# Loads, evictions and matmul order in the head of a fused attention and feed-forward kernel: a second piece of a weight matrix sent from ScalarE, small weights and the last rows of the input loaded later

## The chip, the cores and the metric

The kernel runs on one core of one Trainium2 chip. The metric is the time of one execution on the device in microseconds; three runs were made of the kernel before, and one more execution was profiled.

A core has five engines with a queue of instructions each: TensorE (in the profile PE, its weight loads PEld), VectorE (DVE), ScalarE (ACT), GpSimd (POOL) and SyncE (SP). Each works through its queue in order. SyncE, ScalarE and GpSimd can issue DMAs. An instruction that needs another engine's result, or a landed DMA, waits for a semaphore, and all that is queued behind it on its engine waits too.

## What is computed

One layer on 2048 rows of 448 columns: a normalisation, then a linear attention with 16 heads of 28 columns and a feed-forward part side by side, both added to the input.

```python
xn = _layernorm(x, axis=-1)
return x + _A_ref(xn, A_wqkv, A_w_phi, A_wo) + _B_ref(xn, B_w1, B_w2)

# _A_ref
qkv = (x @ wqkv) ...                       # 16 heads of 28 columns
pq = einsum("bhsd,hdf->bhsf", q, w_phi);  pk = the same of k
phi = concatenate([softmax(p), softmax(-p)])   # of pq and of pk
kv = einsum("bhsf,bhsd->bhfd", phi_k, v);  z = sum of phi_k
o = (phi_q @ kv) / (phi_q @ z + 1e-6);  return o @ wo

# _B_ref
return silu(x @ w1) @ w2                   # 448 -> 1792 -> 448
```

## The kernel before

The program is written as a list of operations with their dependencies. A planner inside the kernel (`schedule`) puts the operations of each engine in order by estimated times; `chain([...])` forces the order of named operations of one engine, and the order of TensorE after the head is written out by hand in `PLAN`. Waits are derived from the dependencies when the instructions are emitted.

**Tiles.** The rows are 16 tiles of 128 (numbers 0 to 15), grouped by four for the feed-forward part (chunks 0 to 3). For each tile `ln_tile` emits the statistics (`bnst`, `bnag`, DVE, L702 and L703), the root of the variance (`ve`, and `rstd`; on ScalarE and DVE for tiles 0 to 3, on POOL for the others, L711 and L713) and the normalisation `xn` (DVE, L717). The normalised tile is then needed with its columns across the partitions. Tiles 0 to 3 are turned on TensorE (`tr0a tr0 tr1 tr2 tr3`, L537) and evicted by ScalarE (`ev0a ev0 ev1 ev2`, L543) or DVE (`ev3`, L547). Tiles 4 to 15 are turned in pairs by DMA transposes from SyncE (`xnT_dma5` for tiles 4 and 5, to `xnT_dma15`).

**The head** is what TensorE does until the first three blocks of the feed-forward part have been fed from tiles 0 to 3: 16 transposes of 128 columns and 72 matmuls of 128 columns. A word such as 01a is block 0, tile 1, part a; part a is the first two steps of the contraction (4 matmuls), part b the third (2 matmuls), and without a letter all three. Blocks 0 and 1 need columns 0 to 511 of `w1`: rows 0 to 255 of it (`w1_0`) for part a, the others (`w1_0r`) for part b. Block 2 needs columns 512 to 1023: rows 0 to 383 (`w1_512`), and for its last matmul of each tile the others (`w1_512r`). `w1` is kept in a part of the tile phT, so its loads are called phT<-in_B_w_dram. Before the head 38 matmuls on ones warm TensorE up (L586).

**After the head** the words of `PLAN` follow: r0, r1, r2 finish the first three blocks; aF and bF are the two halves of a feed-forward block (F7 to F13 are of chunk 1, F21 to F27 of chunk 3), with six and eight matmuls of 512 columns on half of the rows each; av/bv, ak/bk and aq/bq are blocks of the projections; f0 and f1 multiply the map weights `w_phi` into the weights of k (`fold_k`), g0 and g1 into those of q. A fold needs the block-diagonal copies `BD` and `BD0` of the map weights (`bdphi`, `bd0`, POOL, L632 and L636), which come from the loads `wphi` to `wphi3` (issued by POOL, L557), and the transposed weights `wT_dma0` to `wT_dma8` (DMA transposes from SyncE). Its results are read out of two banks by ScalarE (`fold_ref`, last_k) and DVE (`fold_sub`, Wqk, L695). f0 and f1 use the same two banks (6 and 7), so f1 waits for the `fold_sub` of f0.

**Queues around the change.** SyncE issues x0, x1, x2, `w1_0`, `w1_0r`, `w1_512r`, x4, the last third of `w1`, `wv`, x8, then the transposes; ScalarE issues `w1_512` after its first table load. POOL runs its memsets, issues the four loads of the map weights, stands at `bdphi` until they have landed, and goes on with `ve4`.

```python
        chain("bnst0 bnag0 bnst1 bnag1 rstd0 xn0a xn0 rstd1 xn1 bnst2 bnag2 bnst3 bnag3 rstd2 xn2 rstd3 xn3 ev3".split())
        chain("warm_act w1_512 ve0 ve1 ev0a ev0 ev1 ve2 ve3 ev2 silu_table".split())
```

Of the kernel before, what the change touches and what calls it, by code (L numbers as in the profile page):

```python
# [8 lines left out]
ACTF = mybir.ActivationFunctionType  # L9
# [349 lines left out]
SIGNAL = {("act", "pe"): 60.0, ("act", "dve"): 40.0, ("dve", "pe"): 100.0, ("dve", "sp"): 30.0, ("dve", "dve"): 34.0,  # L359
          ("pool", "pe"): 100.0}  # L360
PLAN = """r0 aF3@4 r2 r1 bF3 aF6@0 aF4@6 bF6 bF4 aF5@4 av2@2 av0@0 bv2 bF5 av4@6 bv0 bv4 aF10@2 aF9@0 bF10 f0@6 bF9 aF12@4 aF7@2
aF11@0 f1@6 bF11 bF7 bF12 aF25@0 ak2@6 bF25 bk2 av8@4 av12@2 bv8 ak0@0 bv12 bk0 av10@6 aF22@4 bv10 aF17@2 bF22 av14@6
aF14@0 bF17 bv14 aF18@4 bF14 aF27@6 ak4@2 bF27 bF18 bk4 av6@6 ak6@0 ak8@4 bv6 bk8 bk6 ak12@2 aF8@6 bk12 bF8 aY0@45
aF21@0 aY0 aF23@2 bF21 bF23 ak14@6 bY0 g0@1 bk14 bY0 aF13@0 aF19@2 bF13 aF20@4 bF19 aF24@6 bF20 bF24 ak10@0 g1@3 bk10 K0
K6 K4 aq4@2 K12 aq8@4 bq4 K8 K2 s4 aq0@0 bq8 aq6@2 K14 bq0 bq6 bY1@45 K10 M aY1 aq2@2 aF26@0 s6 bq2 bY1 bF26 aG3@23 aY1
aU2@67 s8 aF15@0 bU2 s0 bF15 aF16@4 bG3 bF16 aU4@01 aq12@6 bU4 bq12 aU3@45 bG3 bU3 s2 aG3 aq10@0 aq14@6 bq10 s10 aW2@45
# [5 lines left out]
def bass_parallel_sum__linear_kernel_hedgehog__dense_activation_silu__prompt_kernel(  # L372
# [10 lines left out]
    S, D, H, DH, FF = 2048, 448, 16, 28, 1792  # L383
# [25 lines left out]
    with es:  # L409
# [38 lines left out]
        w1_sb = flat[:, 0:4 * FF].rearrange("p (k f) -> p k f", k=4)  # L448
# [27 lines left out]
        warm_act = sb("warm_act", [128, 4], F32)  # L476
# [25 lines left out]
        P = _Prog()  # L502
# [96 lines left out]
        def load_w1(c0, c1, eng="sp"):  # L599
            load_rows4(w1_sb[:, :, c0:c1], B_w1, c0, c1, f"w1_{c0}", eng)  # L600
# [2 lines left out]
        load_x(1, 2)  # L603
        load_x(2, 4)
        load(w1_sb[:, 0:2, 0:512], B_w1[0:256, 0:512].rearrange("(k p) f -> p k f", p=128), "w1_0")
        load(w1_sb[:, 2:4, 0:512], bass.AP(B_w1.tensor, B_w1.offset + 256 * FF, [[FF, 128], [64 * FF, 2], [1, 512]]), "w1_0r")
        load_w1(512, 1024, "act")
        load_x(4, 8)
        load_w1(1024, FF)
        load_rows4(wv_sb, A_wqkv, 2 * D, 3 * D, "wv")  # L610
# [88 lines left out]
        def ln_tile(t):  # L699
            xs = x_sb[:, t, :]  # L700
            sl = t % NXN
            P.op("dve", 590, lambda e: e.bn_stats(st6[:, t, :], xs), reads=[xs], writes=[st6[:, t, :]], name=f"bnst{t}", okeys_w=["ln"])  # L702
            P.op("dve", 170, lambda e: e.bn_aggr(mv[:, t, :], st6[:, t, :]), reads=[st6[:, t, :]], writes=[mv[:, t, :]], name=f"bnag{t}",  # L703
                 okeys_w=["ln"])
            if t < 4:
                P.op("act", 220, lambda e: e.activation(ve[:, t:t + 1], mv[:, t, 1:2], ACTF.Sqrt, bias=epst[:]),
                     reads=[mv[:, t, 1:2], epst[:]], writes=[ve[:, t:t + 1]], name=f"ve{t}", table="sqrt", okeys_r=["sq"])
                P.op("dve", 120, lambda e: e.reciprocal(rstd[:, t:t + 1], ve[:, t:t + 1]),
                     reads=[ve[:, t:t + 1]], writes=[rstd[:, t:t + 1]], name=f"rstd{t}")
            else:  # L710
                P.op("pool", 200, lambda e: e.tensor_scalar(ve[:, t:t + 1], mv[:, t, 1:2], EPS_LN, None, ALU.add),  # L711
                     reads=[mv[:, t, 1:2]], writes=[ve[:, t:t + 1]], name=f"ve{t}")
                P.op("pool", 570, lambda e: e.tensor_tensor(rstd[:, t:t + 1], ve[:, t:t + 1], neghalf[:], ALU.pow),  # L713
                     reads=[ve[:, t:t + 1], neghalf[:]], writes=[rstd[:, t:t + 1]], name=f"rstd{t}")

            def norm(dst, c0, c1, dur, tag=""):
                P.op("dve", dur, lambda e: e.tensor_scalar(dst, x_sb[:, t, c0:c1], mv[:, t, 0:1], rstd[:, t:t + 1], ALU.subtract, ALU.mult),  # L717
                     reads=[xs, mv[:, t, 0:1], rstd[:, t:t + 1]], writes=[dst], name=f"xn{t}{tag}")

            dstx = xnT[:, t, :, :]  # L720
            if t >= XN_DMA0:
                norm(xn_sb[:, sl, 0:KF], 0, KF, 370)
                norm(xn_sb[:, sl, KF:512], D - 128, D, 250)
                if t % 2:
                    dma_t(xnT[:, t - 1:t + 1, :, :].rearrange("p i k c -> p (i k) c"),
                          xn_sb[:, sl - 1:sl + 1, :].rearrange("p i c -> p (i c)"), 950.0, f"xnT_dma{t}", 1330.0, lat=850.0)
                return

            def turn_over(k0, k1, b, tag):
                tps = bank16[b][:, 128 * k0:128 * k1].rearrange("p (k c) -> p k c", k=k1 - k0)  # L730
                transposes([(tps[:, kt - k0, :], xn_sb[:, sl, KS[kt]:KS[kt] + 128]) for kt in range(k0, k1)], f"tr{tag}")
                if t < 3:
                    act(dstx[:, k0:k1, :], tps, ACTF.Identity, 128 * (k1 - k0), f"ev{tag}")
                else:
                    copy(dstx[:, k0:k1, :], tps, 128 * (k1 - k0), f"ev{tag}")

            if t == 0:
                norm(xn_sb[:, sl, 0:256], 0, 256, 290, "a")
                norm(xn_sb[:, sl, 256:D], 256, D, 275)
                turn_over(0, 2, 4, "0a")  # L740
                turn_over(2, 4, 5, "0")
            else:
                norm(xn_sb[:, sl, 0:D], 0, D, 390)
                turn_over(0, 4, (7, 4, 5)[t - 1], str(t))

        LOW, HIGH = slice(0, 64), slice(64, 128)

# [266 lines left out]
        def chain(names):  # L1014
            byname = {o.name: o for o in P.ops}
            for a, b in zip(names, names[1:]):
                byname[b].odeps.add(byname[a].id)
                byname[b].odeps -= byname[b].deps
# [3 lines left out]
            ln_tile(t)  # L1022
        fold()
        act(warm_act[:], ones_bf[:, 0:4], ACTF.Silu, 4, "silu_table", table="silu", okeys_w=["sq"])
        chain("bnst0 bnag0 bnst1 bnag1 rstd0 xn0a xn0 rstd1 xn1 bnst2 bnag2 bnst3 bnag3 rstd2 xn2 rstd3 xn3 ev3".split())
        chain("warm_act w1_512 ve0 ve1 ev0a ev0 ev1 ve2 ve3 ev2 silu_table".split())
        byname = {o.name: o for o in P.ops}
        byname["w1_512"].deps.add(byname["warm_act"].id)
        byname["w1_512"].odeps -= byname["w1_512"].deps
        fold_loads()  # L1030

        chunk = [(fp, c) for c in range(NCH) for fp in range(FP)]
# [3 lines left out]

        head = [F(0, 0), F(1, 2), F(2, AUX)]
        seq = []
        for word in "tr0a tr0 tr1 00a 10a 01a 11a 00b 10b 01b 11b tr2 20 21 tr3 02 12 22 03 13 23".split():
            if word[0] == "t":  # L1040
                seq.append(word)
                continue
            f, t = int(word[0]), int(word[1])
            n0 = len(P.ops)
            head[f][0](t * 128, t * 128 + 128, {"": (0, 1, 2), "a": (0, 1), "b": (2,)}[word[2:]])
            for n, o in enumerate(P.ops[n0:]):
                o.name = f"F{word}_{n}"
                seq.append(o.name)
# [4 lines left out]
        block_mask(mask2[:], 2 * DH, 2, KP)  # L1053
        memset(vaug[:, :, :, DH], 1.0, 2150, "vaug1")
        memset(KVm[:], 0.0, 464, "kvm0")
        chain(["vaug1", "kvm0", "wphi", "wphi1", "wphi2", "wphi3"])
        def k_block(t, b0):
            return proj_block(t, b0, True)

# [35 lines left out]
        for word in PLAN.split():  # L1095
# [36 lines left out]
                    finish_pair(t, bank_of[t])  # L1132
            elif kind == "f":
                fold_k(*map(int, arg.split("@")))
            elif kind == "g":
                fold_q(*map(int, arg.split("@")))
            elif kind == "K":
                t0 = int(arg)
                kv(range(t0, t0 + 2))
                if t0 < NEK:  # L1140
                    ones_column(t0, t0 + 2)
            elif kind == "M":
                kvm()
# [111 lines left out]
```

## Time and profile before

| what | value |
|---|---|
| median of the 3 runs | 146.27 us (146.14 to 146.69) |
| the profiled execution, whole | 146.72 us |
| its span, first to last instruction | 145.5 us |
| busy: PE, DVE, ACT, POOL | 97%, 62%, 55%, 52% of the span |
| granted TensorE clock | 1.000 |
| first transposes of the head on PE | 5.07 us |
| r0, the first matmuls after the head | 11.5 us |
| last slices of the span, DMA for the output | PE 0.4 busy in the last fortieth |

The span is counted from the first instruction of the program, and all times of the timeline are microseconds from there. The 1.2 us between the profiled execution and its span lie before the first and after the last instruction. In the page's 40 slices a digit is the busy share in tenths, one slice being 3.64 us:

```profile
PE   7989999899999999999999999999999999999994
DVE  1957899610770059948139999927796374635533
ACT  4567856379997899979896949246530000000000
POOL 8807477720097007799944999992398600000000
DMA  4999969654990000000000059959989999743522
```

### The profile page before, as it was taken

To read this page: it belongs to the slowest core of one execution; us is meant where nothing else is said; L and a number is where in the kernel's file an instruction comes from. 1 tells how busy PE (TensorE), PEld (TensorE's weight loads), DVE (VectorE), ACT (ScalarE), POOL (GpSimd) and SP (SyncE) were. 2 spreads that over 40 slices of the span, in tenths; PEclk is the share of its full clock that TensorE was granted. 3 is DMA by queue.
4 is the path that set the end of the run, shared out by engine and by line. 5 is a ranking of instruction groups with operands and counts; after the bars stand their busy time and mean duration, and the time that the engine had idled before them with its cause. 6 is when DMAs were issued, how large, how long until landed. Compare 5 with 4: busy or idle time off the path is not lost.

```text
span 145.5 us, 4553 instructions
## 1 busy us (share of the span) xinstructions
PE 141.3 (97%) x1968; PEld 83.0 (57%) x1968; DVE 89.5 (62%) x195; ACT 79.5 (55%) x96; POOL 75.2 (52%) x95
## 2 busy tenths in 40 slices
PE   7989999899999999999999999999999999999994
PEld 7785444345444544477787655555555556555773
DVE  1957899610770059948139999927796374635533
ACT  4567856379997899979896949246530000000000
POOL 8807477720097007799944999992398600000000
DMA  4999969654990000000000059959989999743522
GB/s 103 346 342 264 266 142 138 133 106 68 337 293 7 0 2 5 0 0 5 0 5 5 0 89 179 137 109 181 76 163 171 206 196 176 117 76 72 165 95 63
DMA packets 44500, 17.59 MB, mean 121 GB/s; under 512 B 36912, under 2 KB 44096, under 8 KB 44480
## 3 DMA queue, kind: packets, MB, share of 16 engines
q1 hardware_dynamic: 41648, 15.09, 53.0%
q10 hardware_dynamic: 2704, 2.19, 5.4%
q8 instruction: 15, 0.25, 0.7%
q0 software_dynamic: 128, 0.03, 0.1%
q14 instruction: 5, 0.04, 0.1%
HBM read 6.57 MB, written 1.84 MB: 58 GB/s over the span
## 4 chain that ended last, share of the span: by engine, by line
PE 68%; DVE 18%; POOL 5%; DMA 4%; issue 3%; ACT 1%; DVEq 0%; POOLq 0%; ACTq 0%
PE psum L520 68%; DVE Rec L837 7%; DMA Wp<-in_A_w_phi_dram 4%; DVE RA L717 4%; DVE st L702 3%; DVE Rec L838 2%; POOL rstd L713 1%; POOL Wp L557 1%; DVE mv L703 1%; POOL vaug L550 1%; DVE Wqk L695 1%; ACT Ek_sb L543 1%; POOL ve L711 1%; POOL BD L632 0%; DVE Y_sb L949 0%
## 5 line engine op out<-in xcount | busy, mean ns | idle before, releaser
L520 PE MATMUL psum<-xnT,phT 64*128 64x512 bf16 (+1 forms) x428 | 46.9, 350 | 0.6 <-DMA phT<-in_B_w_dram 0.4
L520 PE MATMUL psum<-w_sb,hT 64*128 64x448 bf16 (+4 forms) x455 | 46.5, 341 | 0.0
L837 DVE TENSOR_REDUCE Rec<-Ek_sb 128x32 f32<-128x896 bf16 (+1 forms) x20 | 24.4, 1251 | 18.7 <-ACT Ek_sb L543 18.6
L543 ACT ACTIVATE hT<-psum 128x1024 bf16<-128x1024 f32 x28 | 27.7, 1024 | 11.3 <-PE psum L520 11.2
L520 PEld LDWEIGHTS psum<-w_sb,hT 64*128 64x128 bf16 (+1 forms) x455 | 23.6, 94 | 17.2 <-issue 0.2
L520 PEld LDWEIGHTS psum<-xnT,phT 64*128 64x128 bf16 (+1 forms) x428 | 22.4, 95 | 19.0 <-DMA phT<-in_B_w_dram 0.6
L874 POOL TENSOR_TENSOR RA<-Ek_sb,Rec 128x896 bf16<-128x896 bf16 x16 | 27.1, 1723 | 5.7 <-DVE Rec L838 4.9
L520 PE MATMUL psum<-Wqk,xnT 64*128 64x432 bf16 x224 | 24.4, 342 | 0.0
L543 ACT ACTIVATE Ek_sb<-psum 128x864 bf16<-128x864 f32 x24 | 20.3, 917 | 6.3 <-PE psum L520 4.2
L847 POOL TENSOR_TENSOR Ek_sb<-Ek_sb,Rec 128x896 bf16<-128x896 bf16 x8 | 13.4, 1698 | 17.8 <-DVE Rec L838 17.8
L520 PEld LDWEIGHTS psum<-Wqk,xnT 64*128 64x128 bf16 x224 | 11.1, 94 | 8.2
L543 ACT ACT_TABLE_LOAD x11 | 14.1, 1283 | 1.0 <-PEq L1240 0.8
L847 POOL TENSOR_TENSOR phT<-phT,Rec 128x896 bf16<-128x896 bf16 x8 | 13.4, 1700 | 1.5 <-issue 0.9
L520 PE MATMUL psum<-wv,xnT 64*128 64x448 bf16 x112 | 12.2, 349 | 0.0
L1001 DVE TENSOR_TENSOR x_sb<-psum,x_sb 128x448 bf16<-128x448 f32 (+2 forms) x13 | 7.2, 583 | 7.5 <-PE psum L520 7.4
L702 DVE BATCH_NORM_STATS2 st<-x_sb 128x6 f32<-128x448 bf16 x16 | 9.7, 604 | 3.1 <-DMA x_sb<-in_A_x_dram 3.1
L520 PE MATMUL psum<-wo_sb,vaug 64*128 64x448 bf16 (+2 forms) x102 | 11.3, 338 | 0.0
L717 DVE TENSOR_SCALAR RA<-x_sb,mv,rstd 128x384 bf16<-128x384 bf16 (+4 forms) x29 | 9.0, 349 | 2.3 <-POOL rstd L713 2.1
L980 DVE TENSOR_TENSOR vaug<-psum,rden 128x448 bf16<-128x448 f32 x16 | 9.2, 619 | 0.0
L837 DVE TENSOR_REDUCE Rec<-phT 128x64 f32<-128x1792 bf16 x4 | 8.0, 1990 | 1.8 <-ACT phT L543 1.8
L838 DVE RECIPROCAL Rec<-Rec 128x32 f32<-128x32 f32 (+1 forms) x24 | 8.8, 396 | 0.2
L520 PEld LDWEIGHTS psum<-wv,xnT 64*128 64x128 bf16 x112 | 5.4, 94 | 5.6 <-ACT vaug L543 0.5
(60 smaller groups left out, 108.9 us busy)
## 6 DMA issues: line engine op xcount, KB each, us to landing
out_dram<-x_sb ACTq DMA_DIRECT2D x15, 112.0 KB, 2.4
w_sb<-in_B_w_dram SPq DMA_DIRECT2D x1, 1568.0 KB, 7.9
x_sb<-in_A_x_dram SPq DMA_DIRECT2D x3, 448.0 KB, 6.5
wo_sb<-in_A_wo_dram SPq DMA_DIRECT2D x2, 336.0 KB, 7.5
phT<-in_B_w_dram SPq DMA_DIRECT2D x1, 576.0 KB, 7.8
phT<-in_B_w_dram SPq DMA_DIRECT2D x2, 256.0 KB, 4.4
phT<-in_B_w_dram ACTq DMA_DIRECT2D x1, 384.0 KB, 4.7
wv<-in_A_wqkv_dram SPq DMA_DIRECT2D x1, 336.0 KB, 7.8
```

The source lines that it names most:

```text
L520: r = e.matmul(dst, lhsT, rhs, start=st, stop=sp, skip_group_check=True)
L543: P.op("act", d_act(n), lambda e: e.activation(dst, src, func, scale=scale), reads=[src], writes=[dst], table=table, name=name, **keys)
L550: P.op(eng, d_pool(n, 0.5), lambda e: e.memset(dst, v), writes=[dst], name=name)
L557: P.dma(lambda e: e.dma_start(out=dst, in_=src), n / 280.0, writes=[dst], name=name, eng=eng, lat=lat)
L702: P.op("dve", 590, lambda e: e.bn_stats(st6[:, t, :], xs), reads=[xs], writes=[st6[:, t, :]], name=f"bnst{t}", okeys_w=["ln"])
L717: P.op("dve", dur, lambda e: e.tensor_scalar(dst, x_sb[:, t, c0:c1], mv[:, t, 0:1], rstd[:, t:t + 1], ALU.subtract, ALU.mult), reads=[xs, ...
L837: P.op("dve", 50 + 967 * n, lambda e: e.tensor_reduce(R2, E4, AXL.X, ALU.add), reads=[E4], writes=[R2], name="Ssum")
L838: P.op("dve", 135 + 210 * n, lambda e: e.reciprocal(R2, R2), reads=[R2], writes=[R2], name="Rrec")
L847: P.op("pool", 1700, lambda e: e.tensor_tensor(E3, E3, Rk[:, :, None].broadcast_to([128, 32, DH]), ALU.mult), reads=[E3, Rk], writes=[E3], ...
L874: P.op("pool", 1700, lambda e: e.tensor_tensor(dst, Eq, Rq.rearrange("p (c j) -> p c j", c=CC)[:, :, :, None].broadcast_to([128, CC, 4, DH ...
L980: P.op("dve", 620, lambda e: e.tensor_tensor(o3, U3[:, :, 0:DH], rden[:, uq, :, None].broadcast_to([128, H, DH]), ALU.mult), reads=[U3[:, ...
L1001: P.op("dve", d_dve(cs.stop - cs.start), lambda e: e.tensor_tensor(res[:, cs], ob, addend[:, cs], ALU.add), reads=[ob, addend[:, cs]], wri ...
```

## The change

1. In the head ScalarE issues `w1_0r` (256 KB) where it issued `w1_512` (384 KB); SyncE issues `w1_512` where it issued `w1_0r`.
2. The evictions of tiles 1 and 2 on ScalarE are split in two (`ev1a` and `ev1`, `ev2a` and `ev2`, 256 columns each), TensorE's order in the head is new, and on DVE `bnag3` comes after `xn2`.
3. POOL's loads of the map weights wait for the landing of `w1_512r`, come after the memset kpad, and have `ve4` behind them; `bdphi` and `bd0` come after `rstd9`.
4. SyncE issues x12 (tiles 12 to 15) after `xnT_dma7` rather than after `wT_dma6`; on DVE the `fold_sub` of f0 come before `xn15`.
5. In `PLAN` F8 and F25 change places.

```diff
 PLAN = ...
-aF11@0 f1@6 bF11 bF7 bF12 aF25@0 ak2@6 bF25 bk2 av8@4 av12@2 bv8 ak0@0 bv12 bk0 av10@6 aF22@4 bv10 aF17@2 bF22 av14@6
-aF14@0 bF17 bv14 aF18@4 bF14 aF27@6 ak4@2 bF27 bF18 bk4 av6@6 ak6@0 ak8@4 bv6 bk8 bk6 ak12@2 aF8@6 bk12 bF8 aY0@45
+aF11@0 f1@6 bF11 bF7 bF12 aF8@0 ak2@6 bF8 bk2 av8@4 av12@2 bv8 ak0@0 bv12 bk0 av10@6 aF22@4 bv10 aF17@2 bF22 av14@6
+aF14@0 bF17 bv14 aF18@4 bF14 aF27@6 ak4@2 bF27 bF18 bk4 av6@6 ak6@0 ak8@4 bv6 bk8 bk6 ak12@2 aF25@6 bk12 bF25 aY0@45
...
-        load(w1_sb[:, 2:4, 0:512], bass.AP(B_w1.tensor, B_w1.offset + 256 * FF, [[FF, 128], [64 * FF, 2], [1, 512]]), "w1_0r")
-        load_w1(512, 1024, "act")
+        load(w1_sb[:, 2:4, 0:512], bass.AP(B_w1.tensor, B_w1.offset + 256 * FF, [[FF, 128], [64 * FF, 2], [1, 512]]), "w1_0r", "act")
+        load_w1(512, 1024)
...
-            def turn_over(k0, k1, b, tag):
+            def turn_over(k0, k1, b, tag, cut=None):
...
-                if t < 3:
-                    act(dstx[:, k0:k1, :], tps, ACTF.Identity, 128 * (k1 - k0), f"ev{tag}")
-                else:
-                    copy(dstx[:, k0:k1, :], tps, 128 * (k1 - k0), f"ev{tag}")
+                for a, b, part in ((k0, k1, ""),) if cut is None else ((k0, cut, "a"), (cut, k1, "")):
+                    if t < 3:
+                        act(dstx[:, a:b, :], tps[:, a - k0:b - k0, :], ACTF.Identity, 128 * (b - a), f"ev{tag}{part}")
+                    else:
+                        copy(dstx[:, a:b, :], tps[:, a - k0:b - k0, :], 128 * (b - a), f"ev{tag}{part}")
...
-                turn_over(0, 4, (7, 4, 5)[t - 1], str(t))
+                turn_over(0, 4, (7, 4, 5)[t - 1], str(t), 2 if t < 3 else None)
...
-        chain("bnst0 bnag0 bnst1 bnag1 rstd0 xn0a xn0 rstd1 xn1 bnst2 bnag2 bnst3 bnag3 rstd2 xn2 rstd3 xn3 ev3".split())
-        chain("warm_act w1_512 ve0 ve1 ev0a ev0 ev1 ve2 ve3 ev2 silu_table".split())
+        chain("bnst0 bnag0 bnst1 bnag1 rstd0 xn0a xn0 rstd1 xn1 bnst2 bnag2 bnst3 rstd2 xn2 bnag3 rstd3 xn3 ev3".split())
+        chain("warm_act w1_0r ve0 ve1 ev0a ev0 ev1a ve2 ev1 ve3 ev2a ev2 silu_table".split())
...
-        byname["w1_512"].deps.add(byname["warm_act"].id)
-        byname["w1_512"].odeps -= byname["w1_512"].deps
+        byname["w1_0r"].deps.add(byname["warm_act"].id)
+        byname["w1_0r"].odeps -= byname["w1_0r"].deps
...
-        for word in "tr0a tr0 tr1 00a 10a 01a 11a 00b 10b 01b 11b tr2 20 21 tr3 02 12 22 03 13 23".split():
+        for word in "tr0a tr0 tr1 00a 10a 00b 10b 01a 11a 01b 11b tr2 20 21 02a tr3 12a 22a 02b 12b 22b 03 13 23".split():
...
-        chain(["vaug1", "kvm0", "wphi", "wphi1", "wphi2", "wphi3"])
...
-        chain("x8 wT_dma4 wT_dma5 wT_dma6 x12 wT_dma7 xnT_dma5 xnT_dma7 wT_dma8 xnT_dma9 ...
+        chain("x8 wT_dma4 wT_dma5 wT_dma6 wT_dma7 xnT_dma5 xnT_dma7 x12 wT_dma8 xnT_dma9 ...
...
+        chain(["vaug1", "kvm0", "kpad", "wphi", "wphi1", "wphi2", "wphi3", "ve4"])
+        chain(["rstd9", "bdphi", "bd0", "ve10"])
+        byname = {o.name: o for o in P.ops}
+        byname["wphi"].deps.add(byname["w1_512r"].id)
...
             elif kind == "f":
                 fold_k(*map(int, arg.split("@")))
+                if arg[0] == "0":
+                    xn15 = min(o.id for o in P.ops if o.name == "xn15")
+                    P.ops[xn15].odeps.update(o.id for o in P.ops[n0:] if o.name == "fold_sub")
```

More of the change, by code (lines that the diff above doesn't have):

```diff
@@ L1064, in bass_parallel_sum__linear_kernel_hedgehog__dense_activation_silu__prompt_kernel @@
             ln_tile(t)
-        chain("x8 wT_dma4 wT_dma5 wT_dma6 x12 wT_dma7 xnT_dma5 xnT_dma7 wT_dma8 xnT_dma9 xnT_dma11 xnT_dma13 xnT_dma15 wT_dma0 wT_dma1 wT_dma2 wT_dma3 w2 "
+        chain("x8 wT_dma4 wT_dma5 wT_dma6 wT_dma7 xnT_dma5 xnT_dma7 x12 wT_dma8 xnT_dma9 xnT_dma11 xnT_dma13 xnT_dma15 wT_dma0 wT_dma1 wT_dma2 wT_dma3 w2 "
               "wo0 wor0 wo1 wor1".split())
```

## The prediction

> **What bounds the kernel now.** I read the page's busy times first, then the chain of waits, then the timeline engine by engine, then the list of DMA issues.
>
> ```profile
> PE 141.3 (97%) x1968; PEld 83.0 (57%) x1968; DVE 89.5 (62%) x195; ACT 79.5 (55%) x96; POOL 75.2 (52%) x95
> ```
>
> TensorE is busy for 97% of the span, and from 12 us on nearly every slice is full. The matmuls cannot be made shorter by this change, so it can win only where TensorE stands. On TensorE's timeline I find these places.
>
> ```profile
> 5.07 0.47 PE L537 MATMUL psum<-ident,RA 128*128 128x128 bf16 x4
> 5.71 0.40 PE L537 MATMUL psum<-ident,RA 128*128 128x128 bf16 x4 [0.17 <-DVE RA L717]
> 6.10 1.31 PE L520 MATMUL psum<-xnT,phT 128*128 128x128 bf16 x16
> 7.82 0.62 PE L520 MATMUL psum<-xnT,phT 128*128 128x128 bf16 x8 [0.40 <-DMA phT<-in_B_w_dram]
> 8.27 0.39 PE L537 MATMUL psum<-ident,RA 128*128 128x128 bf16 x4
> 8.50 0.83 PE L520 MATMUL psum<-xnT,phT 128*128 128x128 bf16 x12
> 9.17 0.39 PE L537 MATMUL psum<-ident,RA 128*128 128x128 bf16 x4
> ...
> 26.69 0.81 PE L520 MATMUL psum<-xnT,phT 64*128 64x512 bf16 x6
> 27.88 0.20 PE L520 MATMUL psum<-BD,Y_sb 64*128 64x56 bf16 x1 [0.38 <-DVE Wqk L695]
> ```
>
> Columns: start, duration, engine, line, operation, count, and the idle time before with what ended it. Unhindered, the head's 128-column matmuls start every 0.056 us (8.27 to 8.50 holds 4, 8.50 to 9.17 holds 12). The 16 of the third row need 0.89 us, so 6.10 should lead to 6.99; the next starts at 7.82. So 0.8 us is lost there: 0.25 inside the row, where 01a waits for `ev1` (ScalarE, 6.14 to 6.74, the whole tile in one) and starts at 6.79 instead of 6.55, and 0.56 for the piece `w1_0r`. From 7.82 to the end of the head, 11.4, nothing waits. Later only one wait is large: `aF11` starts at 26.69 and needs 0.65 (8 matmuls of its form take 0.86, 19.23 to 20.09), so `f1` is due at 27.34 and starts at 27.88: 0.54 lost. How that wait came about is in the chain:
>
> ```profile
> 5.16 6.29 DMA Wp<-in_A_w_phi_dram
> 11.52 0.10 issue
> 11.62 0.56 POOL BD L632
> ...
> 26.80 1.04 DVE Wqk L695 x2
> 27.88 13.17 PE psum L520 x144
> ```
>
> The map weights land at 11.45; POOL stood 4.8 us for them (`bdphi`), with `ve4` behind it. From there DVE runs almost unbroken through the statistics and normalisations of tiles 4 to 15 (L702, L717) to the two `fold_sub` at 26.7, which free the banks of `f1`.
>
> **The transfers.** From the list of DMA issues, start (timeline) plus time to landing gives: `w1_0` 2.20+3.8 = 6.0, `w1_512` (ScalarE) 2.33+4.7 = 7.0, `w1_0r` 2.68+5.1 = 7.8, `w1_512r` 3.19+5.0 = 8.2. They land in the order of issue, whichever engine issued, with 0.8 us per 256 KB, 1.0 per 384, 0.4 per 128.
>
> ```profile
> phT<-in_B_w_dram SPq DMA_DIRECT2D x1, 256.0 KB, 5.1
> phT<-in_B_w_dram ACTq DMA_DIRECT2D x1, 384.0 KB, 4.7
> ...
> q10 hardware_dynamic: 313, 0.32, 90.5%
> q1 hardware_dynamic: 48, 0.04, 13.1%
> ```
>
> The last two rows are the packets of ScalarE's (q10) and SyncE's queue (q1) from 4.75 to 5.75 us: for that stretch the earlier issue has the engines almost alone.
>
> **The change, part by part.**
>
> 1. *Loads of the head.* ScalarE now sends `w1_0r` in the place (2.33) of `w1_512`; SyncE sends `w1_512` at 2.68 and `w1_512r` still at 3.19. Each engine issues as many DMAs as before (ScalarE one of 0.43 us, SyncE the same count), so nothing queued behind moves. By order of issue `w1_0` lands at 6.0, `w1_0r` at 6.0+0.8 = 6.8, `w1_512` at 7.8, `w1_512r` at 8.2.
>
> 2. *New head order and split evictions.* 00a 10a (8 matmuls) 6.10 to 6.55; 00b 10b then wait for `w1_0r` until 6.85; from here 72 matmuls follow (88 in the head, less 8 transposes and these 8): 6.85+72 x 0.056 = 10.88. Gates on the way: `ev1a` ends near 6.52 (6.14 and the 0.38 of a 256-column eviction; due 7.07); `ev1`, behind `ve2` (0.29), near 7.05 (due 7.52); `xn2`, now before `bnag3`, near 7.4 (due 7.74); matmul 1 of block 20 at 7.97 against `w1_512` 7.8, its sixth at 8.25 against `w1_512r` 8.2; `xn3` near 8.5 (due 8.86); the copy `ev3` near 9.7 (due 9.87). None holds, some by 0.1 us only. The head ends at 10.88 instead of 11.40: **0.5 us won**, and what follows it finds its inputs: `w1_1024` lands at 12.0 and its rest at 12.5, needed by `aF6` at 13.66-0.5 = 13.1. The split costs ScalarE two more instructions. Two evictions of 256 columns took 0.66 together (5.38), one of 512 took 0.60, so 0.06 us per tile; the idle time of 1.24 us in front of `ev2` hides it, and without that cover block 03 would be late by as much.
>
> 3. *Map weights held until `w1_512r`, `bdphi` after `rstd9`.* POOL waits from 6.8 to 8.2, then issues four DMAs (2.67 us, 3.60 to 6.27 before) until 10.9; queued behind is `ve4`, whose input `bnag4` is ready at 11.07. So POOL costs nothing, and `ve4`, before at 12.16 behind `bdphi`, starts at 11.1: tiles 4 to 11 run about 1.1 us earlier on DVE. The weights land some 6.5 us after issue (6.3 and 6.8 in the list), 15 to 17; `rstd9` ends near 18, `bdphi` and `bd0` take 0.83 more, and `f0` needs them at 23.8. Hidden; without that cover `ve10` would be the next late thing.
>
> 4. *x12 after `xnT_dma7`, `fold_sub` of `f0` before `xn15`.* On SyncE `wT_dma7` moves up to 12.6, `xnT_dma5` is issued at about 14.15, `xnT_dma7` at 15.7 (`xn7` ends at 16.74-1.1), x12 at 17.0; it is moved past three transposes, and `wT_dma8` stays behind it. x12 landed 1.15 us after the transpose ahead of it (17.74 against 16.6). `xnT_dma7` would land at 15.7+3.8 = 19.5, so x12 at **20.7**; with its own old flight of 5.1 it would be 22.1. I take 20.7, since the old flight was spent behind the backlog of 8 us flights that has gone by then. `wT_dma8` follows at 21.3 (0.54 later, as `wT_dma7` did); `f0` needs it at 23.8. From `bnst12` to the end of `xn14` DVE took 4.75 us (20.85 to 25.60), 0.5 of it for `xn11`, which is now done before; the two `fold_sub` take 1.1. They end at 20.7+4.2+1.1 = 26.0, and with x12 at 22.1 at 27.4. `f1` is due at 27.34-0.5 = 26.8. So the 0.54 us **goes** at 20.7 and stays at 22.1. `xn15` slips to 26.6, as late as before (26.19), and its tile is first needed at 34 to 38.
>
> 5. *F8 in place of F25.* Equal counts and shapes on TensorE and ScalarE: nothing. F25 needed tiles 12 to 15 at 30.69, 0.5 after the last transpose landed (30.15); F8 needs tiles 4 to 7.
>
> Later work hangs on TensorE's own order: the DVE stretch from 78.8 to 93.5 in the chain starts from `exp` of a block that TensorE releases at 77, so it moves along.
>
> Sum: span 145.5-0.5-0.54 = 144.4. The profiled run took 146.72 with 1.2 outside its span; the median of the runs is 146.27, 0.45 below it. I take the difference from the median: **145.2 us**.
>
> **Rivals.**
>
> *The queues share (chance 0.12).* If both queues alternate on the engines, `w1_0` and `w1_0r`, now equally large and issued 0.13 apart, both land at 6.8. Then 00a starts at 6.85 and 80 matmuls follow to 11.33: 0.07 won, with `f1` 0.6, **145.7**. For it: both have packets in flight together; against it: the 313 to 48 above. The Trainium skill, DMA: Bandwidth & Descriptors, section "Queues, rings and completion order", says each DMA engine takes turns between the queues it has work for, a packet at a time; in that microsecond the trace does not agree.
>
> *x12 a little late (0.14).* At 22.1 the wait at `f1` stays: head only, **145.7**.
>
> *Slower: x12 much late (0.10).* DVE works in order, so `fold_sub` stands behind tiles 12 to 14. The other loads of x12's size took 6.5 and 8.4 us: at 6.5 it lands at 23.5, `fold_sub` ends at 28.8, `f1` waits 2.0 instead of 0.54: 146.27-0.5+1.5 = **147.2**. It decides from a landing at 22.5 on. Against it: those two stood behind 2 MB of other loads.
>
> *Gain given back (0.08).* TensorE waits for DVE at 93.5 already (0.2 us); if DVE there does not move along, the time stays at **146.2**. This is also the case where the changed queue has no effect in the head.
>
> *More (0.10).* `w1_0` landed 1.6 after x2 (4.4) where 0.8 would do, just while POOL issued the map weights. If those caused it, all pieces land 0.8 earlier and the head is bound by its evictions: end near 10.6, **144.9**. Against it: nothing of q0 moved before 7.5. The Trainium skill's same page, section "Latency and other measured facts", gives the descriptor rings of POOL's DMAs as a best guess for why two DMA engines are often slower; no view here settles that.
>
> **Numbers.** Forecast 0.46, the rivals as given. A measurement here tells 0.5%, 0.73 us, so 145.54 and 147.0 are the borders. Faster: forecast and "more", 0.56; same: "share", "a little late" and "given back", 0.34; slower: 0.10. The range 144.7 to 146.5 leaves out the slower rival and little else; the likeliest case alone spans 144.9 (both waits gone whole) to 145.5 (0.3 us of them left).
>
> **What would show it.** `w1_0r` lands below 7.0 and before `w1_512`; the wait of 0.40 before the 8 matmuls is 0.3 or less; `r0` starts at 11.0 instead of 11.5; `ve4` on POOL at 11.1; x12 lands before 21.5, the wait before `f1` is gone, and `bF11` starts 1.0 us earlier than 28.10. The forecast is wrong if `w1_0` lands later than 6.1, if x12 lands after 22, or if a new wait of TensorE above 0.3 us stands behind 30 us.

## The result, and the profile after

| | median | runs | ratio to before |
|---|---|---|---|
| before | 146.22 us (145.84 to 146.78) | 22 | |
| after | 146.75 us (146.37 to 147.64) | 22 | 1.0043 [1.0031, 1.0055] |

The change makes the kernel slower by 0.43%. That is less than the 0.5% (0.73 us) which the prediction called measurable, but its interval lies above 1, and 145.2 us was forecast. The profiled executions of both kernels have the same span, 145.5 us (146.74 us whole after, 146.72 before).

The page of the changed kernel, part 1, busy times:

```profile
PE 141.1 (97%) x1968; PEld 83.6 (57%) x1968; DVE 90.7 (62%) x195; ACT 79.7 (55%) x98; POOL 75.0 (52%) x95
```

TensorE has the same instructions and, within 0.2 us, the same busy time; ScalarE has the two more evictions. DVE is busy for 1.2 us more with the same 195 instructions: an operation must have become longer. Of the changed kernel, the timeline of TensorE in the head and around `f1` (start, duration, engine, line, operation, count, idle time before it and what ended it):

```profile
6.76 1.50 PE L520 MATMUL psum<-xnT,phT 128*128 128x128 bf16 x24 [0.65 <-ACT ve L706]
...
25.66 1.68 PE L520 MATMUL psum<-xnT,phT 64*128 64x512 bf16 x14
27.86 0.20 PE L520 MATMUL psum<-BD,Y_sb 64*128 64x56 bf16 x1 [0.52 <-DVE Wqk L695]
```

The wait inside the head for `w1_0r` is gone; all 24 matmuls of blocks 0 and 1 on tiles 0 and 1 run in one row. But the first of them starts at 6.76, not at 6.10. The row puts that wait down to a `ve` on ScalarE, on which these matmuls do not depend; what they wait for is `w1_0`, landed at 6.63, 0.13 us earlier (0.13 also in e2, e6 and e8 below, and the rows of e6 and e8 name the DMA). In these traces the semaphore of a transfer gets sixteen updates, and the landing is the last: fourteen of those of `w1_0` had come by 5.89, the last two at 6.57 and 6.63. The issues with their flights (size, time to landing), after:

```profile
phT<-in_B_w_dram SPq DMA_DIRECT2D x1, 256.0 KB, 4.4
...
phT<-in_B_w_dram ACTq DMA_DIRECT2D x1, 256.0 KB, 4.5
```

Issued at 2.21 and 2.35, `w1_0` lands at 6.63 and `w1_0r` at 6.88. `r0` starts at 11.32 instead of 11.49: 0.17 us won. And `f1`, which started at 27.88, starts at 27.86: nothing of it is left. It waits for `fold_sub` as before. The timelines of DVE and of POOL, after:

```profile
25.26 0.60 DVE L717 TENSOR_SCALAR RA<-x_sb,mv,rstd 128x384 bf16<-128x384 bf16 x2
26.46 0.32 DVE L717 TENSOR_SCALAR RA<-x_sb,mv,rstd 128x128 bf16<-128x128 bf16 x1 [0.60 <-POOL rstd L713]
26.68 1.12 DVE L695 TENSOR_TENSOR Wqk<-psum,last_k 128x432 bf16<-128x432 f32 x2
27.71 1.54 DVE L717 TENSOR_SCALAR RA<-x_sb,mv,rstd 128x384 bf16<-128x384 bf16 x1
```

```profile
11.30 0.26 POOL L711 TENSOR_SCALAR ve<-mv 128x1 f32<-128x1 f32 x1
...
25.79 0.56 POOL L713 TENSOR_TENSOR rstd<-ve,neghalf 128x1 f32<-128x1 f32 x1
26.83 1.21 POOL L550 MEMSET Ek_sb<- 128x256 bf16 x1 [0.48 <-DVE RA L717]
27.63 1.51 POOL L550 MEMSET phT<- 128x256 bf16 x1
```

Every `xn` is two instructions, one of 384 columns and one of 128 (the x2 of the first row are those of `xn14`). So it was before, where both halves of `xn15`, and ahead of them a wait of 0.60 us, stood in front of the two `fold_sub`:

```profile
26.19 0.60 DVE L717 TENSOR_SCALAR RA<-x_sb,mv,rstd 128x384 bf16<-128x384 bf16 x2 [0.60 <-POOL rstd L713]
26.71 1.12 DVE L695 TENSOR_TENSOR Wqk<-psum,last_k 128x432 bf16<-128x432 f32 x2
```

Of `xn15` after the change, the half of 384 columns stands behind the two `fold_sub` (27.71), but the half of 128 columns stands in front of them (26.46), and it waits 0.60 us for the last `rstd`. The added lines take `min(...)` over the operations called `xn15`, so they order only the first of the two, and the planner put the second one ahead. So `fold_sub` still ends behind a wait for tile 15. The other half takes 1.54 us instead of 0.37, and these are the 1.2 us more of DVE's busy time.

The chain of waits, after, up to this place (start, duration, what):

```profile
18.45 0.53 POOL BD L632
18.98 0.29 POOL BD L636
...
20.38 0.57 POOL rstd L713
21.05 0.60 DVE RA L717 x2
21.65 0.55 DVE st L702
...
25.79 0.57 POOL rstd L713
...
26.68 1.13 DVE Wqk L695 x2
27.86 13.17 PE psum L520 x144
```

The chain no longer leads from the landing of the map weights to `ve4`. It starts at the landing of `w1_512r` (8.38), for which POOL's loads of the map weights wait, and passes `ve4` (11.30). From there it leads over `bdphi` and `bd0` (18.45, 18.98), which now stand on POOL ahead of `ve10`, to the `rstd` and `xn` of tile 11 (20.38, 21.05), and from there over the statistics and normalisations of tiles 12 to 15, which all come after. DVE's rows show the waits for POOL, and `bnst12`, the statistics of tile 12, as the last:

```profile
20.14 0.60 DVE L717 TENSOR_SCALAR RA<-x_sb,mv,rstd 128x384 bf16<-128x384 bf16 x2 [0.69 <-POOL rstd L713]
21.05 0.60 DVE L717 TENSOR_SCALAR RA<-x_sb,mv,rstd 128x384 bf16<-128x384 bf16 x2 [0.31 <-POOL rstd L713]
21.57 0.63 DVE L702 BATCH_NORM_STATS2 st<-x_sb 128x6 f32<-128x448 bf16 x1
```

Two releases coincide here: `xn11` makes DVE free for `bnst12` at 21.57, and x12 lands at 21.54. Behind 30 us nothing new appears: TensorE waits 0.18 us before 41.05 and 0.05 us before 93.54, and at the same two places it waited 0.17 and 0.23 us before.

### The profile page after: what moved, and what is told of

It reads as the page before. It is cut to its first block, busy times and chain, and to the rows that moved or that the text cites. A ratio compares the mean times of both kernels' runs of the same rounds, so it can differ in the third digit from the quotient of the medians.

```text
span 145.5 us, 4557 instructions
## 1 busy us (share of the span) xinstructions
PE 141.1 (97%) x1968; PEld 83.6 (57%) x1968; DVE 90.7 (62%) x195; ACT 79.7 (55%) x98; POOL 75.0 (52%) x95
## 3 DMA queue, kind: packets, MB, share of 16 engines
HBM read 6.57 MB, written 1.84 MB: 58 GB/s over the span
## 4 chain that ended last, share of the span: by engine, by line
PE 79%; POOL 6%; DVE 6%; DMA 4%; SPq 1%; issue 1%; DVEq 0%; POOLq 0%
PE psum L520 79%; DMA phT<-in_B_w_dram 4%; POOL rstd L713 3%; DVE RA L717 2%; DVE st L702 2%; POOL Wp L557 2%; SPq L557 1%; POOL ve L711 1%; DVE Wqk L695 1%; DVE mv L703 1%; POOL BD L632 0%; DVE x_sb L1002 0%; POOL BD L636 0%; DVEq L1217 0%; POOLq L1217 0%
## 5 line engine op out<-in xcount | busy, mean ns | idle before, releaser
L543 ACT ACTIVATE hT<-psum 128x1024 bf16<-128x1024 f32 x28 | 27.7, 1025 | 11.1 <-PE psum L520 10.9
L520 PEld LDWEIGHTS psum<-w_sb,hT 64*128 64x128 bf16 (+1 forms) x455 | 23.8, 94 | 17.0 <-issue 0.2
L520 PEld LDWEIGHTS psum<-xnT,phT 64*128 64x128 bf16 (+1 forms) x428 | 22.5, 95 | 18.6 <-ACT ve L706 0.8
L717 DVE TENSOR_SCALAR RA<-x_sb,mv,rstd 128x384 bf16<-128x384 bf16 (+4 forms) x29 | 10.2, 387 | 2.5 <-POOL rstd L713 2.4
```

Of the source, the lines that this page charges most:

```text
L520: r = e.matmul(dst, lhsT, rhs, start=st, stop=sp, skip_group_check=True)
```

## The experiments

In every profile of this study, whatever the variant, the span is the start of `f1` plus 117.6 us (117.58 to 117.64). So all that the variants do is decided before `f1`, and two times tell it: the start of `r0`, and the start of `f1`. Without a wait between the two TensorE needs 15.85 us (11.40 to 27.25 in the profile of e5). "Lost" is start of `f1` minus start of `r0` minus 15.85. It is longer than the idle time in the row of `f1`, since the profile models the ends of matmuls and here starts are compared. Landings are those of the semaphores in the trace; `bnst12` is given where x12 is sent late, and the end of `fold_sub` is that of the second one.

| kernel | r0 | x12 landed | bnst12 starts | fold_sub ends | f1 | lost | span |
|---|---|---|---|---|---|---|---|
| before | 11.49 | 17.74 | | 27.83 | 27.88 | 0.54 | 145.5 |
| e5, before again | 11.40 | 17.77 | | 26.96 | 27.25 | 0 | 144.9 |
| after | 11.32 | 21.54 | 21.57 | 27.80 | 27.86 | 0.69 | 145.5 |
| e9, after again | 10.99 | 21.80 | 21.83 | 28.06 | 28.12 | 1.28 | 145.7 |
| e1, parts 3 to 5 alone | 11.48 | 21.76 | 21.78 | 27.50 | 27.55 | 0.22 | 145.2 |
| e2, parts 1 and 2 alone | 10.89 | 17.73 | | 27.17 | 27.23 | 0.49 | 144.8 |
| e3, both halves of xn15 behind | 11.06 | 21.69 | 21.71 | 27.03 | 27.09 | 0.18 | 144.7 |
| e4, one queue | 12.04 | 21.91 | 22.41 | 28.63 | 28.69 | 0.80 | 146.3 |
| e10, one queue and both halves | 11.94 | 21.84 | 22.33 | 27.65 | 27.79 | 0 | 145.4 |
| e6, x12 back | 10.90 | 18.29 | | 26.74 | 27.09 | 0.34 | 144.7 |
| e7, e3 with early map weights | 10.73 | 22.62 | 22.64 | 27.96 | 28.02 | 1.44 | 145.6 |
| e8, e7 with x12 back | 11.21 | 17.83 | | 26.58 | 27.06 | 0 | 144.7 |
| e11, e3 with x12 back | 10.90 | 18.18 | | 26.48 | 26.96 | 0.21 | 144.6 |

From the start of `bnst12` to the end of `fold_sub` it is 5.32 us in e3, e7 and e10, where both halves of `xn15` stand behind, and 6.22 to 6.23 in after, e9 and e4, where one stands in front: **the order costs 0.9 us**. Where `fold_sub` ends late, `f1` starts 0.05 or 0.06 us behind it.

Each ratio below is to runs of the kernel before that were measured beside that group of experiments (medians 146.37 us for e1 to e4, 146.33 for e5 to e8, 146.69 for e9 to e11), with its 95% interval; it can differ by up to 0.3% from the ratio of the two medians.

The theory after the result: the order on DVE (half of `xn15` ahead of `fold_sub`), together with the late tiles 12 to 15, takes back what the head wins. Its rivals: the head itself wins nothing, because the two queues share the engines; or the later x12 alone is enough to lose it.

**e1 and e2: the change in two.** e1 has the loads of the map weights, x12, `fold_sub` and PLAN as after and the head as before; e2 has the head as after (loads, split evictions, order) and all else as before.

> The kernel before with parts 3 to 5 of the change alone (map weights and x12 later, bdphi after rstd9, fold_sub before the first half of xn15, F8 and F25 exchanged); loads, evictions and order of the head as before. Theory A (the changed kernel loses at f1, because the two fold_sub stand on VectorE behind the second half of xn15, which hangs on x12 landing near 21.5 us): f1 starts at 27.8 to 28.0 as in the changed kernel although the head ends 0.2 us later, x12 lands at 21 to 22, and the time is that of the changed kernel, 0.3 to 0.6 us above before. Rival B (the loss comes from the new loads and order of the head): the time is that of before or below it.

> The kernel before with parts 1 and 2 alone (w1_0r from ScalarE, new order and split evictions of the head). Theory A: w1_0 and w1_0r share the engines and land together near 6.6 to 6.9, r0 starts at 11.3 (0.2 us earlier than before), f1 waits as much longer as the head is shorter, and the time is within 0.2 us of before. Rival B: the time is 0.3 to 0.6 us above before, like the changed kernel's.

e1: 146.68 us, 1.0016 [0.9992, 1.0039]. e2: 145.95 us, 0.9958 [0.9936, 0.9979]. So the head alone wins, 0.42%, and the rest alone wins nothing. Neither expectation was right in full: in e1 `f1` started at 27.55, earlier than 27.8, and of e2 neither theory nor rival came true, as `w1_0` landed at 6.20 and the head gained more than 0.2 us. In e2 `r0` is 0.6 us earlier than in the profile of before, while `f1` still loses 0.49 us: there `fold_sub` stands behind both halves of `xn15`, as it did before. The timeline of DVE in e1 shows the order of the changed kernel in another form:

```profile
25.99 0.60 DVE L695 TENSOR_TENSOR Wqk<-psum,last_k 128x432 bf16<-128x432 f32 x1
26.67 0.31 DVE L717 TENSOR_SCALAR RA<-x_sb,mv,rstd 128x128 bf16<-128x128 bf16 x1
26.90 0.60 DVE L695 TENSOR_TENSOR Wqk<-psum,last_k 128x432 bf16<-128x432 f32 x1
27.41 2.05 DVE L717 TENSOR_SCALAR RA<-x_sb,mv,rstd 128x384 bf16<-128x384 bf16 x1
```

Here the half of `xn15` fell between the two `fold_sub`, and the second one ends at 27.50.

**e3: only the order on DVE.** The changed kernel, with both instructions of `xn15` behind `fold_sub`:

```diff
-                    xn15 = min(o.id for o in P.ops if o.name == "xn15")
-                    P.ops[xn15].odeps.update(o.id for o in P.ops[n0:] if o.name == "fold_sub")
+                    for o in [o for o in P.ops if o.name == "xn15"]:
+                        o.odeps.update(f.id for f in P.ops[n0:] if f.name == "fold_sub")
```

> The changed kernel with both halves of xn15 behind the fold_sub of f0, not the first alone; VectorE's order differs in nothing else. Theory A: fold_sub starts near 25.9 instead of 26.7, the wait before f1 (0.68 us) is gone or below 0.1, bF11 starts 0.6 us earlier, the memset of POOL no longer overlaps xn15, and the time is 0.5 to 0.7 us below the changed kernel's, 146.0 to 146.3. Rival B (f1 is not what sets the end): the time stays at 146.7.

Measured: 145.96 us (145.76 to 146.12), 0.9964 [0.9947, 0.998]. Two lines turn 0.43% lost into 0.36% won; the intervals are far apart. DVE and TensorE in e3:

```profile
25.41 0.59 DVE L717 TENSOR_SCALAR RA<-x_sb,mv,rstd 128x384 bf16<-128x384 bf16 x2
25.92 1.11 DVE L695 TENSOR_TENSOR Wqk<-psum,last_k 128x432 bf16<-128x432 f32 x2
26.95 0.59 DVE L717 TENSOR_SCALAR RA<-x_sb,mv,rstd 128x384 bf16<-128x384 bf16 x2
```

```profile
25.71 1.48 PE L520 MATMUL psum<-xnT,phT 64*128 64x512 bf16 x12
27.09 0.20 PE L520 MATMUL psum<-BD,Y_sb 64*128 64x56 bf16 x1
```

x12 landed 0.15 us later than in the profile of after and `bnst12` started 0.14 later, and still `fold_sub` ends 0.77 us earlier, directly behind `xn14`, without the wait for the last `rstd`. The wait before `f1` falls from 0.68 to 0.08 us. So `f1` starts 0.77 us earlier: some 0.61 is this wait, 0.26 the earlier `r0`, and 0.10 is lost on the way, at `f0`.

**e4: the loads of the head on one queue.** The changed kernel with `w1_0r` sent by SyncE behind `w1_0` (and taken out of ScalarE's order, which is not shown); the order of the pieces is the same.

```diff
-        load(w1_sb[:, 2:4, 0:512], ... "w1_0r", "act")
+        load(w1_sb[:, 2:4, 0:512], ... "w1_0r")
```

> The changed kernel with all pieces of w1 sent by SyncE in the order in which the head needs them (w1_0, w1_0r, w1_512, w1_512r), none by ScalarE. If the two queues share the engines (theory A): w1_0 lands alone, at 5.3 to 6.0 instead of 6.6, and w1_0r near 6.3 to 6.8; the head ends 0.4 to 0.7 us earlier than in the changed kernel, but f1 still starts near 27.9, its wait is 0.4 to 0.7 us longer, and the time is that of the changed kernel within 0.2 us. Rival (the DMAs are served in order of issue whatever the queue, and w1_0 was late by chance): w1_0 lands as in the changed kernel.

Measured: 147.41 us, 1.006 [1.0042, 1.0077]. `w1_0` landed at 5.74, as theory A had it, but `w1_0r` 2.05 us behind it, and `r0` slipped to 12.04: neither expectation held for the head. Twelve of the sixteen updates of `w1_0r` had come by 6.49, the last four at 6.87 to 7.79. This looked as if ScalarE's queue landed the piece earlier. Since the wait at `f1` was in it as well, I took that wait away later, in e10.

**e5: before, once more.** The same program as before, in another profiled execution.

> The kernel before once more, for a second look at its trace. Theory A: the profiled execution of before (146.72 us) was one of the slower ones; most runs are near 146.2. In a look near 146.2 the wait before f1 is 0.0 to 0.2 us instead of 0.54, with the map weights landed about 0.5 us earlier or DVE ahead by as much. Rival: the 0.5 us between that look and the median lie elsewhere (the head, the end, or outside the span), and f1 waits 0.5 us here too.

Measured: 146.12 us. Of it, the timelines of DVE and of TensorE at `f1`:

```profile
25.33 0.60 DVE L717 TENSOR_SCALAR RA<-x_sb,mv,rstd 128x384 bf16<-128x384 bf16 x2 [0.59 <-POOL rstd L713]
25.85 1.11 DVE L695 TENSOR_TENSOR Wqk<-psum,last_k 128x432 bf16<-128x432 f32 x2
```

```profile
25.73 1.68 PE L520 MATMUL psum<-xnT,phT 64*128 64x512 bf16 x14
27.25 0.19 PE L520 MATMUL psum<-BD,Y_sb 64*128 64x56 bf16 x1
```

In this execution of the kernel before there is **no wait at `f1`** at all: the map weights landed earlier than in the first profile (9.73 to 11.45 against 10.43 to 12.21; the third, the last that `bdphi` waits for, by 0.89 us), DVE was earlier by as much (`bnst12` at 19.99 against 20.85), and `fold_sub` ended 0.29 us before TensorE came. The first profile, 146.72 us, lies at the upper end of the runs (145.84 to 146.78 around a median of 146.22).

**e6: only x12.** The changed kernel with x12 where it was before, and the half of `xn15` still ahead of `fold_sub`.

```diff
-        chain("x8 wT_dma4 wT_dma5 wT_dma6 wT_dma7 xnT_dma5 xnT_dma7 x12 wT_dma8 ...
+        chain("x8 wT_dma4 wT_dma5 wT_dma6 x12 wT_dma7 xnT_dma5 xnT_dma7 wT_dma8 ...
```

> The changed kernel with x12 issued ahead of wT_dma7 again, as before; fold_sub still behind the second half of xn15. Theory A (f1 is late because DVE's work on tiles 12 to 15 starts only when x12 lands at 21.5): x12 lands near 18, fold_sub ends 0.8 to 1.2 us earlier, f1 waits less than 0.1 us, and the time falls by 0.5 to 0.7 us to 146.0 to 146.2. Rival (the loss is due to the map weights' delay or to bdphi between rstd9 and ve10): f1 still waits 0.5 us or more, time above 146.5.

Measured: 145.92 us, 0.996 [0.9942, 0.9978]. With x12 at 18.29 `fold_sub` ends at 26.74 in spite of the order. The statistics of tile 12 now fill the time in which DVE waits for POOL's `rstd` of tiles 10 and 11 (0.69 and 0.31 us idle after, 0.18 in e6). So either remedy is enough (the order at least where x12 lands near 21.7, as in e3), and the loss of the changed kernel needs both: the late x12 and the half of `xn15` in front. A new wait of 0.33 us at 19.83 (for a copy on ScalarE) takes part of the head's gain.

**e7 and e8: is the delay of the map weights needed?** e7 is e3 with the map weights loaded at once as before, but `bdphi` still behind `rstd9`; e8 is e7 with x12 back ahead of `wT_dma7`.

```diff
-        chain(["vaug1", "kvm0", "kpad", "wphi", "wphi1", "wphi2", "wphi3", "ve4"])
+        chain(["vaug1", "kvm0", "wphi", "wphi1", "wphi2", "wphi3", "ve4"])
...
-        byname["wphi"].deps.add(byname["w1_512r"].id)
```

> As e3 (both halves of xn15 behind fold_sub), and the map weights are loaded at once as before, not after w1_512r; bdphi still after rstd9. Theory A: the map weights carry 27 KB and do not set when the pieces of w1 land; the head ends where it ended in e3 and e2 within 0.2 us, and the time is that of e3, 145.9 to 146.1. Rival (their loads slow one DMA engine while the head's pieces arrive): w1_0 and w1_0r land 0.3 to 0.6 us later than in e3, the time is 0.3 us or more above e3's.

> e7 with x12 ahead of wT_dma7 as before: the head of the change, map weights and x12 loaded early, bdphi after rstd9, both halves of xn15 behind fold_sub. Theory A: DVE is ahead on all tiles, f1 does not wait at all, the head ends at 10.8 to 11.1, and the time is 145.6 to 145.9, 0.3 to 0.5% below before. Rival (x12's transfer so early delays the transposes that feed av4, F10 or f0): TensorE waits elsewhere before 28 us and the time is above e3's.

e7: 146.93 us (145.73 to 147.75), 1.0013 [0.9982, 1.0044]. e8: 145.69 us (145.44 to 145.94), 0.9942 [0.9918, 0.9966]. In the head the early map weights did no harm: e7 has the earliest `r0` of all, 10.73. The time is not that of e3, though, for a reason that neither expectation named: in the profiled execution x12 flew 5.5 us instead of 3.9 to 4.0, and then even the right order on DVE does not help. DVE and TensorE in e7:

```profile
22.64 0.63 DVE L702 BATCH_NORM_STATS2 st<-x_sb 128x6 f32<-128x448 bf16 x1 [1.52 <-DMA x_sb<-in_A_x_dram]
```

```profile
25.71 1.03 PE L520 MATMUL psum<-xnT,phT 64*128 64x512 bf16 x8
28.02 0.20 PE L520 MATMUL psum<-BD,Y_sb 64*128 64x56 bf16 x1 [1.27 <-DVE Wqk L695]
```

DVE in e8, with x12 at 17.83, and TensorE:

```profile
25.46 1.12 DVE L695 TENSOR_TENSOR Wqk<-psum,last_k 128x432 bf16<-128x432 f32 x2 [0.50 <-ACT last_k L543]
26.50 0.60 DVE L717 TENSOR_SCALAR RA<-x_sb,mv,rstd 128x384 bf16<-128x384 bf16 x2
```

```profile
25.76 1.46 PE L520 MATMUL psum<-xnT,phT 64*128 64x512 bf16 x12
27.06 0.19 PE L520 MATMUL psum<-BD,Y_sb 64*128 64x56 bf16 x1
```

Now `fold_sub` waits for ScalarE's copy (`last_k`), DVE has time to spare, and `f1` starts as soon as TensorE comes. e8 beats both kernels.

**e9: after, once more.** The changed kernel in another profiled execution.

> A second profile of the changed kernel. If the order on VectorE is the cause, the first fold_sub of f0 ends after the second half of xn15 has run again, and f1 waits 0.4 us or more (it started at 27.86 in the first profile) wherever x12 lands at 21.3 or later; the first half of xn15 takes 1.4 us or more beside the memset again. If the first profile was an odd execution, f1 starts below 27.4 and the wait is under 0.2.

Measured: 146.97 us. DVE again:

```profile
26.71 0.31 DVE L717 TENSOR_SCALAR RA<-x_sb,mv,rstd 128x128 bf16<-128x128 bf16 x1 [0.60 <-POOL rstd L713]
26.94 1.12 DVE L695 TENSOR_TENSOR Wqk<-psum,last_k 128x432 bf16<-128x432 f32 x2
27.98 1.54 DVE L717 TENSOR_SCALAR RA<-x_sb,mv,rstd 128x384 bf16<-128x384 bf16 x1
```

The head is as good here as forecast (`r0` at 10.99), yet `f1` starts at 28.12, later than in any profile of before. A better head makes the wait longer, 0.93 us, and not the kernel faster. TensorE also lost 0.35 us at `f0`, which was due at 23.82 and started at 24.17, for `wT_dma8` (landed 24.03); that loss lies under the one at `f1`.

**e10: one queue, without the wait at `f1`.** e3 with the edit of e4.

> The kernel e3 (both halves of xn15 behind fold_sub) with all first pieces of w1 sent by SyncE in the order in which they are needed. If the second queue is what lands w1_0r early: w1_0r lands at 7.6 to 7.9, r0 starts near 12.0 against 11.06 in e3, and the time is 0.5 to 1.0 us above e3, so a ratio near 1.001. If only the order of the pieces matters: w1_0r by 7.0, r0 at 11.1, ratio 0.996.

Measured: 146.55 us, 0.9992 [0.9976, 1.0009]. Neither expectation came true whole. `w1_0r` landed at 6.66, as early as from ScalarE's queue, and still `r0` started at 11.94. TensorE in e10:

```profile
8.12 0.45 PE L520 MATMUL psum<-xnT,phT 128*128 128x128 bf16 x5
9.21 0.79 PE L520 MATMUL psum<-xnT,phT 128*128 128x128 bf16 x11 [0.64 <-DMA phT<-in_B_w_dram]
```

After five matmuls of block 20 the sixth waits: for `w1_512r`, issued at 3.71 instead of 3.19, since SyncE now issues one DMA more ahead of it, at about 0.5 us each, and landed at 9.16 (9.22 in e4) instead of 7.92 to 8.38. So the second engine's part in the gain is at least this issue slot of 0.5 us; the queue as such did not land `w1_0r` earlier here. What the landing lost beyond the slot, 0.3 to 0.8 us, stays open (in e10 the last of the sixteen updates came at 9.16, the one ahead of it at 8.41). The Trainium skill, DMA: Bandwidth & Descriptors, section "Rules for kernel authors", says that spreading DMAs over the issuing engines brings no bandwidth and only saves sequencer issue time. The trace of e10 agrees, with `w1_0r` at 6.66 from one queue and at 6.22 to 6.88 from two. That of e4, with 7.79, does not decide it: why the last updates of `w1_0r` came so late there stays unexplained.

**e11: e3 with x12 back.** Against e8 only the delay of the map weights is left in.

> The changed kernel with both halves of xn15 behind fold_sub and x12 back ahead of wT_dma7; against e8 only the map weights are still held until w1_512r. If the delay of the map weights helps the head or the tiles 4 to 11: ratio 0.991 to 0.994. If it does nothing once x12 is early: as e8, 0.9942 within 0.0015. If it costs through x12's neighbours: 0.996 or more.

Measured: 145.81 us (145.63 to 146.24), 0.9944 [0.9922, 0.9966]; e8 had 0.9942. Once x12 is early, the delay of the map weights does nothing that shows.

## Why the prediction failed, step by step

**The step that failed: "They end at 20.7+4.2+1.1 = 26.0 ... So the 0.54 us goes at 20.7".** Of the two terms of the sum, the 0.5 us of the head came true (0.46 on the means of `r0`), and the 0.54 us at `f1` is the one that failed: in its place 0.69 us is lost up to `f1` in one profile of the changed kernel and 1.28 in the other. The step has three errors.

- *The order.* It let `fold_sub` follow directly behind `xn14`, as the change was worded. The 5.3 us (4.2 and 1.1) are right where the order is so: 5.32 in e3. In the changed kernel it is 6.23, by the 0.60 us wait for the last `rstd` and the half of `xn15`. The diff shows the `min(...)`, and DVE's rows of before show each `xn` as two instructions; together they said it. "DVE runs almost unbroken" up to `fold_sub` also passed over the wait of 0.60 us that stood there before. With the order of e3, `fold_sub` would have ended in the profile of after at 21.57 + 5.32 = 26.9, and TensorE was due at 11.32 + 15.85 = 27.2: no wait. With x12 as late as it was, this is the error that decided.
- *The start of tile 12*, 20.7, was mis-sized twice. x12 landed at 21.54 to 21.91 in six profiles and at 22.62 in e7 (after: issued at 17.56 instead of 17.0, flight 4.0 us instead of 3.7). And DVE was not ready for it sooner: "`xn11`, which is now done before" ran at 21.05 to 21.57. `bdphi` and `bd0`, 0.82 us on POOL, were called hidden, but they now stand ahead of `ve10`: `xn9` ran 1.0 us earlier than before (18.77 against 19.75), `xn11` only 0.4 (21.05 against 21.46), with 1.0 us of idle time on DVE between. In e7 x12 alone was late (1.52 us idle), in e4 and e10 POOL alone. The rival "x12 a little late" had 22.1 and the wait unchanged, which is the mechanism of the result in weaker form; it expected the head's 0.5 us to survive. They could not: `fold_sub` hangs from x12, POOL and DVE, so `f1` does not move with the head any more. That was missed in the rival and in the sum. The rival "x12 much late" had this mechanism, but said that it decides from a landing at 22.5 on; that follows from 5.3 us, and with the 6.23 us of the changed kernel it decides from 27.83 - 6.23 = 21.6 on, just where x12 landed.
- *The base.* "I take the difference from the median" subtracted a wait seen in one execution of 146.72 us from a median of 146.27. The execution of e5, near the median, has no wait at `f1`, so there was nothing to win at that place in such a run, and much to lose: `f1` at 27.86 and 28.12 after, against 27.25. This is how a change with an unchanged profile span, 145.5, can be slower by 0.53 us at the median. The median run of before is 0.1 us above that of e5, and so should wait some 0.1 us there (an estimate, with the head and all behind `f1` as in e5).

**The head: mechanism and size right.** `w1_0r` lands below 7.0 and ahead of `w1_512` (7.97), and the wait before the 8 matmuls is gone. With the new order and the two queues `r0` started at 10.73 to 11.32 in eight profiles, mean 11.00, where 11.0 was forecast; in the three with the old head at 11.40 to 11.49. The profiled execution of after was the worst of the eight, with both pieces late, as the rival "the queues share" had it. Over the eight, the two landings lie 0.24 to 0.74 us apart: between that rival and the 0.8 us of the forecast. The rival's mechanism of turns between the queues is neither shown nor excluded by that. That the head's gain is there in the runs too, e2 shows.

**The map weights: times right, worth nothing.** POOL issued them from 8.68 to 11.27 and `ve4` started at 11.30 (11.1 forecast); they landed at 16.2 to 17.4 (15 to 17 forecast), hidden. "So POOL costs nothing" is not quite right: the input of `ve4` was ready at 10.82, and it stood behind the issues for some 0.4 us more. The earlier DVE came up to tile 9 and was lost again at tiles 10 to 12. The rival "more", which had the early map weights delay the pieces in the head by 0.8 us, finds no support: loaded early, they left `w1_0` landing at 5.80 to 6.41 (e2, e7, e8), and held back at 5.70 to 6.63.

**`wT_dma8` was priced at nothing with a landing at 21.3.** It landed at 23.55 after and 24.03 in e9, its flight 5.4 and 5.5 us instead of 3.1. The cover, `f0` at 23.8, was almost used up, and in e9 it was gone (0.35 us lost); so it was in e3, where `wT_dma8` landed at 23.86 and 0.10 us was lost at `f0`.

**F8 for F25, and all behind `f1`: nothing, as forecast.** The 117.6 us hold in every variant. What would show the forecast wrong was stated as `w1_0` later than 6.1 or x12 after 22; `w1_0` at 6.63 hit the first, but e9, with `w1_0` at 5.89, loses more, so it was not the cause of the loss.

## What to carry to other kernels

Where an order is forced by name, count the instructions that bear the name, and look for the one that is left out; an engine that works in order waits for the worst of them. Before a wait is subtracted from a median, look whether an execution near the median has it. When a transfer is moved later to make room, work out how late it may land before it takes the place of the wait that is to go: here x12 came 3.8 us later than before and used up all the time that `fold_sub` had to spare.

## What the hardware showed that was not expected

**A memset on POOL held an operation of DVE.** The half of `xn15` with 384 columns takes some 0.37 us in e3 (0.59 for both halves, overlapped). Beside POOL's memset of phT it took 1.54 us after, in e4 and in e9, 1.56 in e6 and 2.05 in e1 (where it began 0.43 us ahead of that memset, beside the one of Ek_sb), and it ended about 0.1 us behind the end of the memset of phT each time: 29.26 against 29.14 after. DVE and POOL in e6:

```profile
26.66 1.56 DVE L717 TENSOR_SCALAR RA<-x_sb,mv,rstd 128x384 bf16<-128x384 bf16 x1
```

```profile
26.59 1.53 POOL L550 MEMSET phT<- 128x256 bf16 x1
```

`fold_sub`, which reads the banks of TensorE, ran beside the other memset at its usual length (1.12 us for two). The Trainium skill, SBUF — State Buffer, section "SBUF: two separate sides", says that DVE in its two-port modes and GpSimd lock one port pair against each other for whole instructions. The trace agrees in that DVE was held to the memset's end while the memset kept its length (1.51 us after, 1.54 in e3); in which mode DVE ran, no view shows. It cost TensorE nothing that shows here, as tile 15 is needed late.

**Landings of one program vary by 0.3 to 0.9 us between two executions**: `w1_0` landed at 6.63 and 5.89 in the two profiles of after, the four map weights 0.30 to 0.89 us apart in the two of before. Over the variants `w1_0` lay at 5.70 to 6.63 with the new head, and the flight of the late x12 was 3.9 to 5.5 us. The runs spread most in e1 (146.0 to 148.0) and e7 (145.7 to 147.8), where `fold_sub` hangs on x12, and least in e3 (145.8 to 146.1), e4 (147.2 to 147.7) and e8 (145.4 to 145.9); that the landing of x12 makes the spread is likely, but no run shows it.
